# Denominators and variances of a fused attention and MLP kernel leave TensorE in short pieces on more rows

## The chip, the core and the metric

The kernel runs on one core of a Trainium2 chip. The metric is device time in microseconds (us). A core has five engines that run side by side, each through its own queue in order: TensorE (PE; its weight loads are shown apart, as PEld), VectorE (DVE), ScalarE (ACT), GpSimd (POOL) and SyncE (SP), which issues most of the DMA transfers.

## The reference

Three stages run one after the other on 4 batches of a sequence of 1088. First, linear attention with 4 heads of 32, whose features are the 64 products of two projections to 8:

```python
def phi(x):
    a = np.einsum('rd,bhsd->bhsr', S1, x)
    b = np.einsum('rd,bhsd->bhsr', S2, x)
    return np.einsum('bhsi,bhsj->bhsij', a, b).reshape(*x.shape[:-1], r * r)
q_p, k_p = (phi(q), phi(k))
kv = np.einsum('bhsf,bhsd->bhfd', k_p, v)
z = np.sum(k_p, axis=2)
num = np.einsum('bhsf,bhfd->bhsd', q_p, kv)
den = np.einsum('bhsf,bhf->bhs', q_p, z)[..., None] + 1e-06
return (num / den).astype(np.float32)
```

Second, on the 128 channels: a two-dimensional FFT, a layer norm and an MLP of 128 to 512 to 128.

```python
X = np.fft.fft(np.fft.fft(x, axis=1), axis=2)
u = x + np.real(X).astype(np.float32)
mu = np.mean(u, axis=-1, keepdims=True)
var = np.mean((u - mu) ** 2, axis=-1, keepdims=True)
un = (u - mu) / np.sqrt(var + 1e-06)
return u + np.maximum(un @ w_ch1, 0.0) @ w_ch2
```

Third, a gated MLP of 128 to 1024 to 128: `h = relu(x @ w_in)`, a convolution of three taps along the sequence, a sigmoid of it as the gate, and `(h * gate) @ w_out`.

## The kernel before

Channels lie on the 128 partitions and the sequence along the free axis, in pieces of 364, 364 and 360. Per batch the stages are `load_attn`, `attn`, `fft`, `moe1` and `moe2`; the loop over the batches stands at the end of `tile_fwd`. It runs nothing yet: each operation is only recorded (class `Program`, `record`), and `issue` then hands all of them to the engines in the order of a table of numbers, `ORDER`, lines 43 to 115. So every instruction of the profile has line 150, the call in `issue`, and rows are told apart by the names of their tiles. The table interleaves the batches: while one is in `moe2`, the next is in `attn` and `fft`. An engine runs its part strictly in that order, so an instruction that waits holds up all behind it.

Attention. `q`, `k` and `v` are loaded (`v` on 121 rows, since the sequence is cut into 9 tiles of 121), with weights and constants; 64-bit weights go through `load64`, which brings a `raw` tile of two shared slots and converts it to f32 in `em` on ACT and VectorE. `kab` and `qab` are the projections, `kp` and `qa` their products. In batch 0 the products of q are made from two wide projections (`sq_sb`) with three `acc` banks to share; in the others q's projections go through DRAM (`qd`) to be spread over the partitions. `kv_ps` sums keys times values, with a column of ones in `v` for the denominators' weights `z`. The denominators, `den`, are 8 matmuls of 32 rows by 273 columns, four column groups for the four quarters of the sequence; of every 32 rows, four (one for each head) hold a value. ACT adds eps (`rd`). In batch 0 VectorE takes the reciprocal of 128x273, and 4 matmuls with a selection matrix spread it over the partitions (`rb`). In batches 1 to 3 four transfers bring the 16 useful rows to 112x39 (`rr`), VectorE takes the reciprocal, one transfer writes it to DRAM (`rrd`) and four read it back, each head's over 32 partitions (`x`). Then `x` is multiplied by `num`.

Layer norm. `norm` in `moe1` squares the centred `u` (`cen`, `sq`), and 4 matmuls with `ones_v` give the variances, of which one row in 32 is needed (`var`); ACT takes the root (`rs`, 128x272). In batch 0 VectorE takes the reciprocal and GpSimd spreads it. In the others a transfer brings the four rows to 32x34 (`rt`), then comes the reciprocal, a transfer to DRAM (`rtd`) and one back over all partitions (`y`), which `down` multiplies into `ch`. From that come `yh` and `yl`, a value's upper part and its rest, which the matmuls `z` of `moe2` read.

`idle` are 48 matmuls on a tile of zeros (96 records, as an f32 matmul is recorded twice), which the table puts between the others.

## Time and profile before

| | us |
|---|---|
| median of 3 timed runs (267.41 to 267.97) | 267.42 |
| the profiled run | 265.54 |
| its span, in which the rows stand | 263.8 |
| TensorE busy | 254.1 (96%) |
| VectorE busy | 234.4 (89%) |
| ACT busy | 184.7 (70%) |
| GpSimd busy | 5.7 (2%) |

The profile is of one execution; its span runs from the first to the last instruction. PE is a matmul, PEld a weight load, which runs beside the matmuls. "x16" is a count of records. Idle time before a row stands in brackets with what ended it. A chain of waits is followed back from the last instruction.

### The profile page before, as it was taken

What the parts mean: (1) busy time and instruction counts of PE and PEld (TensorE: products, weight loads), DVE (VectorE), ACT (ScalarE), POOL (GpSimd) and SP (SyncE); (2) the same over time, 40 slices, a digit from 0 to 9 for tenths busy, and PEclk for the clock granted to TensorE, in tenths of its full rate; (3) what the DMA queues carried; (4) which work ended last, traced back from release to release, by engine and by line L of the source; (5) the groups of instructions that cost most, each with busy time, mean ns of one, the idle gap of its engine ahead of it and who ended that gap; (6) DMA issues with size and microseconds to landing.
All of it is one profiled execution on the core that took longest, in us unless ns stands there. A gap on an engine that the chain in (4) does not pass through costs nothing.

```text
span 263.8 us, 4314 instructions
## 1 busy us (share of the span) xinstructions
PE 254.1 (96%) x1644; PEld 198.5 (75%) x1644; DVE 234.4 (89%) x354; ACT 184.7 (70%) x330; POOL 5.7 (2%) x15
## 2 busy tenths in 40 slices
...
GB/s 234 276 388 306 178 188 209 155 207 214 107 130 262 65 14 120 0 132 126 79 10 2 60 0 87 97 20 0 0 2 28 1 40 105 0 0 28 59 0 85
DMA packets 9360, 26.48 MB, mean 100 GB/s; under 512 B 2360, under 2 KB 3896, under 8 KB 9084
## 3 DMA queue, kind: packets, MB, share of 16 engines
...
q0 software_dynamic: 400, 2.67, 3.0%
...
HBM read 23.00 MB, written 3.13 MB: 99 GB/s over the span
## 4 chain that ended last, share of the span: by engine, by line
PE 81%; DMA 9%; DVE 4%; ACT 4%; issue 1%; SPq 1%; ACTq 0%
PE z L150 27%; PE acc L150 18%; PE ch L150 11%; PE spec L150 4%; DVE t L150 4%; PE qab_ps L150 3%; PE kv_ps L150 3%; PE p_ps L150 3%; DMA v<-va 3%; PE num L150 3%; PE idle L150 2%; PE kab_ps L150 2%; DMA q<-qT 2%; DMA qd<-qab 2%; DMA raw<-w 2%; PE den L150 2%
## 5 line engine op out<-in xcount | busy, mean ns | idle before, releaser
L150 DVE SCALAR_TENSOR_TENSOR t<-h,cw_sb,t 128x1087 f32<-128x1087 f32 x64 | 83.6, 1339 | 0.8 <-ACT t L150 0.3
L150 PE MATMUL acc<-t,wo_sb 128*128 128x364 f32 (+1 forms) x192 | 68.8, 470 | 0.2 <-DVE t L150 0.2
L150 ACT ACTIVATE h<-z 128x364 f32<-128x364 f32 (+1 forms) x96 | 41.4, 474 | 16.7 <-PE z L150 16.0
L150 DVE TENSOR_TENSOR t<-t,h 128x1088 f32<-128x1088 f32 (+2 forms) x34 | 41.0, 1219 | 4.3 <-ACT t L150 4.2
L150 PEld LDWEIGHTS acc<-t,wo_sb 128*128 128x128 f32 x192 | 34.6, 189 | 11.3 <-issue 1.0
L150 ACT ACTIVATE t<-h,cw_sb 128x1088 f32<-128x1088 f32 x32 | 38.6, 1208 | 2.0 <-PE var L150 1.7
L150 ACT ACTIVATE t<-t 128x1088 f32<-128x1088 f32 (+2 forms) x34 | 35.5, 1056 | 4.1 <-DVE t L150 3.7
L150 PE MATMUL z<-yh,win_hi 128*128 128x364 f32 (+1 forms) x96 | 34.3, 382 | 0.0
L150 PE MATMUL ch<-hid,w_sb 128*128 128x364 f32 (+1 forms) x96 | 33.7, 470 | 0.0
L150 PE MATMUL z<-yh,win_lo 128*128 128x364 f32 (+1 forms) x96 | 33.1, 361 | 0.0
L150 PE MATMUL z<-yl,win_hi 128*128 128x364 f32 (+1 forms) x96 | 31.7, 350 | 0.0
L150 ACT ACTIVATE hid<-z 128x364 f32<-128x364 f32 (+1 forms) x48 | 21.7, 476 | 12.1 <-PE z L150 11.2
L150 PEld LDWEIGHTS ch<-hid,w_sb 128*128 128x128 f32 x96 | 17.2, 189 | 6.9 <-ACT hid L150 0.7
L150 PEld LDWEIGHTS z<-yh,win_hi 128*128 128x128 f32 x96 | 17.9, 188 | 4.8 <-ACT t L150 1.0
L150 PE MATMUL z<-uh,w_hi 128*128 128x364 f32 (+1 forms) x48 | 17.8, 395 | 2.3 <-ACT hid L150 2.3
L150 PEld LDWEIGHTS z<-yh,win_lo 128*128 128x128 f32 x96 | 18.0, 189 | 2.3
L150 PEld LDWEIGHTS z<-yl,win_hi 128*128 128x128 f32 x96 | 17.8, 188 | 1.8
L150 PEld LDWEIGHTS idle<-still 128*128 128x128 f32 x96 | 15.4, 214 | 4.1 <-issue 1.3
L150 PE MATMUL idle<-still 128*128 128x128 f32 x96 | 17.2, 305 | 1.2 <-DVE still L150 1.2
L150 PE MATMUL z<-uh,w_lo 128*128 128x364 f32 (+1 forms) x48 | 17.8, 377 | 0.0
L150 PE MATMUL z<-ul,w_hi 128*128 128x364 f32 (+1 forms) x48 | 16.5, 367 | 0.0
L150 PE MATMUL p_ps<-mats_sb,parts 128*32 128x128 f32 (+1 forms) x160 | 15.0, 277 | 0.0
(115 smaller groups left out, 388.2 us busy)
## 6 DMA issues: line engine op xcount, KB each, us to landing
...
v<-va SPq DMA_DIRECT2D x4, 561.5 KB
...
```

The lines of the kernel that those rows point to most:

```text
L150: fn(*args, **kw)
```

## The change

Rows that hold nothing are filled. A piece of the denominators' quarter (91 of 273 columns, `DJ = 3`) goes to its own row for each head: the weights `z` become a wider tile, in which the piece's window of 32 columns starts one column further left, and 24 matmuls add into the same 32 rows. Twelve of 32 rows then hold values, in 91 columns. `rd` and its reciprocal are 128x91 in all batches and go straight to DRAM; the four `rr` transfers are gone, and the four `x` transfers read three runs a quarter. In batch 0 the spreading takes 12 matmuls with three selection matrices, so `mats` grows from 320 to 448 KB. Likewise the variances of batches 1 to 3 take 16 matmuls of 68 columns (`VJ = 4`) with a shifted window of `one_v`; root and reciprocal are 128x68, and the `rt` transfer is gone. `v` is loaded on 128 rows (594 KB in place of 561.5), of which the matmuls still use 121. The idle matmuls are 24, and every number of `ORDER` is new.

```diff
-P = dict(near=(0,), kvt=(0, 1, 3), hs=(), hlo=4, xb=2, sq=(0,), rpe=(0,), rnear=(), up=(0,), mo=12, hid=7, idle=48)
+P = dict(near=(0,), kvt=(0, 1, 3), hs=(), hlo=4, xb=2, sq=(0,), rpe=(0,), up=(0,), mo=12, hid=7, idle=24)
...
+DJ = 3
+DW = QW // DJ
+VJ = 4
+ZW = 32 + DJ - 1
...
 ORDER = [
-    30, 31, 32, 33, 0, 1, 2, 3, 34, 4, 5, 85, 9, 6, 7, 8, 10, 16, 24, 14, 12, 35, 36, 37, 94, 91, 13, 23, 19, 83, 15, 22, 38, 95, 96, 25, 225, 87, 11,
...
+    72, 32, 33, 9, 0, 8, 63, 34, 35, 36, 67, 1, 73, 2, 37, 38, 39, 40, 41, 3, 42, 43, 4, 5, 6, 7, 19, 30, 16, 23, 61, 13, 15, 44, 11, 45, 74, 21, 191,
...
     ones_v = cst.tile([128, 32], F32, name="ones_v")
     V.memset(ones_v, 1.0 / D)
+    one_v = cst.tile([128, 63], F32, name="one_v")
+    V.memset(one_v, 0.0)
+    V.memset(one_v[:, 31:32], 1.0 / D)
     vks = []
     for i in range(2):
         vks.append(cst.tile([128, 128], F32, name=f"vk{i}"))
...
     kvz = []
     for i in range(2):
         t = cst.tile([128, 2, 64], F32, name=f"kv{i}")
-        z = cst.tile([128, 64], F32, name=f"z{i}")
+        z = cst.tile([128, 2 * ZW], F32, name=f"z{i}")
         V.memset(t, 0.0)
         V.memset(z, 0.0)
         kvz.append((t, z))
...
     def load_attn(b):
         k_sb[b] = at.tile([D, NKT * KT], F32, tag="k", name=f"k{b}")
         nc.sync.dma_start(k_sb[b], kT[b])
-        v_sb[b] = at.tile([KT, NKT, NH, HD + 1], F32, tag="v", name=f"v{b}")
+        v_sb[b] = at.tile([128, NKT, NH, HD + 1], F32, tag="v", name=f"v{b}")
         nc.sync.dma_start(v_sb[b], va[b])
         q_sb[b] = at.tile([D, SP], F32, tag="q", name=f"q{b}")
         nc.sync.dma_start(q_sb[b], qT[b])
-    mats_sb = cst.tile([D, 5, D], F32, name="mats_sb")
-    eye_sb, sel_sb, cen_sb, c_sb, s_sb = (mats_sb[:, i] for i in range(5))
+    mats_sb = cst.tile([D, 4 + DJ, D], F32, name="mats_sb")
+    eye_sb, cen_sb, c_sb, s_sb, *sel_sb = (mats_sb[:, i] for i in range(4 + DJ))
     tab_hi = cst.tile([128, 8, NK], F32R, name="tab_hi")
     tab_lo = cst.tile([128, 8, NK], F32R, name="tab_lo")
     tab_end = cst.tile([96, 4, NK], F32R, name="tab_end")
...
                     for hp in range(2):
                         T.matmul(
                             kv_ps[64 * hp:64 * hp + HD + 1, 64 * h2:64 * h2 + 64],
-                            vt[:, t, 2 * hp + h2, :],
+                            vt[:KT, t, 2 * hp + h2, :],
                             kp[hp][:, t, h2].rearrange("p i j -> p (i j)"),
                             start=(t == 0),
                             stop=(t == NKT - 1),
...
                     T.matmul(
                         kv_ps[:, hp * 66:(hp + 1) * 66],
                         kp[hp][:, t].rearrange("p h i j -> p (h i j)"),
-                        vt[:, t, 2 * hp:2 * hp + 2, :].rearrange("p h d -> p (h d)"),
+                        vt[:KT, t, 2 * hp:2 * hp + 2, :].rearrange("p h d -> p (h d)"),
                         start=(t == 0),
                         stop=(t == NKT - 1),
                     )
...
         for h2 in range(2):
             r = slice(64 * h2, 64 * h2 + 64)
             V.tensor_copy(kv[r, :, 32 * h2:32 * h2 + 32], kvv[h2][:, :, 0:32])
-            V.tensor_copy(zz[r, h2:h2 + 35:34], kvv[h2][:, :, 32])
+            V.tensor_copy(zz[r, DJ - 1 + DJ * h2:DJ + DJ * h2 + ZW + 2 * DJ:ZW + 2 * DJ], kvv[h2][:, :, 32])
         for hp in range(0 if b in P["sq"] else 2):
             V.tensor_tensor(qa[hp], qa[hp], qb[hp], op=ALU.mult)
         den = bank(f"den{b}", "mm")
         for hp in range(2):
             for c in range(4):
-                T.matmul(
-                    den[32 * c:32 * c + 32, :QW],
-                    zz[:, 32 * hp:32 * hp + 32],
-                    qa[hp][:, c * QW:(c + 1) * QW],
-                    start=(hp == 0),
-                    stop=(hp == 1),
-                )
-        rd = at.tile([128, QW], F32, tag="rd", name=f"rd{b}")
-        A.activation(rd, den[:, :QW], AF.Identity, bias=eps_d)
+                for j in range(DJ):
+                    o = ZW * hp + DJ - 1 - j
+                    T.matmul(
+                        den[32 * c:32 * c + 32, :DW],
+                        zz[:, o:o + 32],
+                        qa[hp][:, c * QW + j * DW:c * QW + (j + 1) * DW],
+                        start=(hp == 0 and j == 0),
+                        stop=(hp == 1 and j == DJ - 1),
+                    )
+        rd = at.tile([128, DW], F32, tag="rd", name=f"rd{b}")
+        A.activation(rd, den[:, :DW], AF.Identity, bias=eps_d)
+        V.reciprocal(rd, rd)
         x = xs[b] = ff.tile([128, SP], F32, tag="x", name=f"x{b}", bufs=P["xb"])
         xq = x.rearrange("p (c n) -> p c n", c=4)
         if b in P["rpe"]:
-            V.reciprocal(rd, rd)
             for c in range(4):
                 p = bank(f"rb{b}_{c}", "mm")
-                T.matmul(p[:, :QW], sel_sb[32 * c:32 * c + 32, :], rd[32 * c:32 * c + 32, :], start=True, stop=True)
+                for j in range(DJ):
+                    r = slice(32 * c, 32 * c + 32)
+                    T.matmul(p[:, j * DW:(j + 1) * DW], sel_sb[j][r], rd[r], start=True, stop=True)
                 A.copy(xq[:, c, :], p[:, :QW])
-        elif b in P["rnear"]:
-            V.reciprocal(rd, rd)
-            for c in range(4):
-                r = rd[32 * c:32 * c + NH, :]
-                nc.sync.dma_start(xq[:, c, :], r.unsqueeze(1).to_broadcast([NH, HD, QW]))
         else:
-            rr = at.tile([4 * NH * 7, QW // 7], F32, tag="rr", name=f"rr{b}")
+            rrd = dr.tile([128, DW], F32, tag="rrd", name=f"rrd{b}")
+            nc.sync.dma_start(rrd, rd)
             for h in range(NH):
-                nc.sync.dma_start(rr[28 * h:28 * h + 28, :], rd[h:h + 97:32, :])
-            V.reciprocal(rr, rr)
-            rrd = dr.tile([NH, SP], F32, tag="rrd", name=f"rrd{b}")
-            nc.sync.dma_start(rrd.rearrange("h (s n) -> (h s) n", n=QW // 7), rr)
-            for h in range(NH):
-                src = bass.AP(rrd.tensor, rrd.offset + h * SP, [[0, HD], [1, SP]])
-                nc.sync.dma_start(x[HD * h:HD * h + HD, :], src)
+                src = bass.AP(rrd.tensor, rrd.offset + h * DJ * DW, [[0, HD], [32 * DW, 4], [1, QW]])
+                nc.sync.dma_start(xq[HD * h:HD * h + HD], src)
         for i in range(3):
             n = bank(f"num{b}_{i}", "mm")
             for hp in range(2):
...
                 T.matmul(c[:, :w], cen_r, ul[:, o:o + w], start=False, stop=True)
                 A.activation(sq[:, o:o + w], c[:, :w], AF.Square)
             vp = bank(f"var{b}")
-            for c in range(4):
-                T.matmul(vp[32 * c:32 * c + 32, :VW], ones_v, sq[:, c * VW:(c + 1) * VW], start=True, stop=True)
-            rs = ln.tile([128, VW], F32, tag="rs", name=f"rs{b}")
-            A.activation(rs, vp[:, :VW], AF.Sqrt, bias=eps_d)
             if b in P["near"]:
+                for c in range(4):
+                    T.matmul(vp[32 * c:32 * c + 32, :VW], ones_v, sq[:, c * VW:(c + 1) * VW], start=True, stop=True)
+                rs = ln.tile([128, VW], F32, tag="rs", name=f"rs{b}")
+                A.activation(rs, vp[:, :VW], AF.Sqrt, bias=eps_d)
                 V.reciprocal(rs, rs)
                 yq = y.rearrange("p (c n) -> p c n", c=4)
                 for c in range(4):
                     G.partition_broadcast(yq[:, c, :], rs[32 * c:32 * c + 1, :])
             else:
-                rt = ln.tile([32, VW // 8], F32, tag="rt", name=f"rt{b}")
-                nc.sync.dma_start(rt, rs[0:97:32, :])
-                V.reciprocal(rt, rt)
-                rtd = dr.tile([32, VW // 8], F32, tag="rtd", name=f"rtd{b}")
-                nc.sync.dma_start(rtd, rt)
-                nc.sync.dma_start(y, bass.AP(rtd.tensor, rtd.offset, [[0, D], [1, SEQ]]))
+                n = VW // VJ
+                for c in range(4):
+                    for j in range(VJ):
+                        o = c * VW + j * n
+                        T.matmul(vp[32 * c:32 * c + 32, :n], one_v[:, 31 - j:63 - j], sq[:, o:o + n], start=(j == 0), stop=(j == VJ - 1))
+                rs = ln.tile([128, n], F32, tag="rt", name=f"rt{b}")
+                A.activation(rs, vp[:, :n], AF.Sqrt, bias=eps_d)
+                V.reciprocal(rs, rs)
+                rtd = dr.tile([128, n], F32, tag="rtd", name=f"rtd{b}")
+                nc.sync.dma_start(rtd, rs)
+                src = bass.AP(rtd.tensor, rtd.offset, [[0, D], [32 * n, 4], [1, VW]])
+                nc.sync.dma_start(y.rearrange("p (c n) -> p c n", c=4), src)
         up(0)
         norm()
...
-_SEL = np.kron(np.ones((4, 1)), np.kron(np.eye(32, NH), np.ones((1, HD)))).astype(np.float32)
+_SEL = [
+    np.kron(np.ones((4, 1)), np.kron(np.eye(32)[:, j:j + DJ * NH:DJ], np.ones((1, HD)))).astype(np.float32)
+    for j in range(DJ)
+]
...
+    vv = np.concatenate([vv, np.zeros((NB, 128 - KT) + vv.shape[2:], v.dtype)], axis=1)
...
-        "mats": np.concatenate([np.eye(D, dtype=np.float32), _SEL, _CEN, _C, _S], axis=1),
+        "mats": np.concatenate([np.eye(D, dtype=np.float32), _CEN, _C, _S, *_SEL], axis=1),
```

SyncE at the start, before (raw tiles hold 64-bit weights; w is that of the first MLP, twice, win that of the second):

```order
L150 DMA raw_78<-srep 128x16
L150 DMA q_108<-qT 128x1092
L150 DMA raw_109<-w 128x512
L150 DMA k_106<-kT 128x1089
L150 DMA raw_112<-w 128x512
L150 DMA v_107<-va 121x1188
L150 DMA mats_sb<-mats 128x640
L150 DMA raw_114<-win 128x512
L150 DMA q_259<-qT 128x1092
L150 DMA raw_116<-win 128x512
L150 DMA k_257<-kT 128x1089
```

SyncE at the start after:

```order
L157 DMA raw_110<-w 128x512
L157 DMA raw_78<-srep 128x16
L157 DMA q_109<-qT 128x1092
L157 DMA k_107<-kT 128x1089
L157 DMA raw_115<-win 128x512
L157 DMA mats_sb<-mats 128x896
L157 DMA v_108<-va 128x1188
L157 DMA raw_113<-w 128x512
L157 DMA k_258<-kT 128x1089
L157 DMA q_260<-qT 128x1092
L157 DMA raw_117<-win 128x512
```

w and srep, the vectors of the projections, have changed places; half of win has moved ahead of mats and v, and the second w behind v.

TensorE at the start, before, up to the first kv matmul:

```order
L150 MATMUL qab_ps_1_2_0_143<-q_108,sq_sb 128x364
L150 MATMUL idle<-still 128x128 x4
L150 MATMUL qab_ps_0_0_1_134<-q_108,sq_sb 128x364
L150 MATMUL qab_ps_0_2_0_137<-q_108,sq_sb 128x364
L150 MATMUL idle<-still 128x128 x2
L150 MATMUL qab_ps_1_2_1_144<-q_108,sq_sb 128x364
L150 MATMUL idle<-still 128x128 x3
L150 MATMUL qab_ps_0_2_1_138<-q_108,sq_sb 128x364
L150 MATMUL idle<-still 128x128
L150 MATMUL kv_ps_131<-kp_1_130,v_107 33x64
```

TensorE after, from its first matmul on; the row that follows is the first kv matmul:

```order
L157 MATMUL idle<-still 128x128 x13
L157 MATMUL qab_ps_0_0_0_134<-q_109,sq_sb 128x364
L157 MATMUL qab_ps_1_0_0_140<-q_109,sq_sb 128x364
L157 MATMUL kab_ps_0_128<-sab_sb,k_107 121x64 x5
L157 MATMUL qab_ps_1_0_1_141<-q_109,sq_sb 128x364
L157 MATMUL qab_ps_1_1_0_142<-q_109,sq_sb 128x364
L157 MATMUL kab_ps_0_128<-sab_sb,k_107 121x64 x3
L157 MATMUL qab_ps_0_1_0_136<-q_109,sq_sb 128x364
L157 MATMUL qab_ps_0_2_0_138<-q_109,sq_sb 128x364
L157 MATMUL kab_ps_1_129<-sab_sb,k_107 121x64
L157 MATMUL qab_ps_0_1_1_137<-q_109,sq_sb 128x364
L157 MATMUL qab_ps_1_2_0_144<-q_109,sq_sb 128x364
```

kv begins after eight of the twelve qab matmuls in place of all twelve, behind 13 idle matmuls at the start in place of eight.

TensorE at the end of moe1 of batch 0 and the beginning of moe2 (the z matmuls that read yh), before:

```order
L150 MATMUL ch_2_210<-hid_2_3_209,w_sb 128x360
L150 MATMUL z_0_0_364_217<-yh_175,win_hi 128x364
L150 MATMUL z_0_4_0_236<-yh_175,win_hi 128x364
L150 MATMUL z_0_4_0_236<-yh_175,win_lo 128x364
L150 MATMUL z_0_0_364_217<-yh_175,win_lo 128x364
L150 MATMUL z_0_0_364_217<-yl_176,win_hi 128x364
L150 MATMUL z_0_4_0_236<-yl_176,win_hi 128x364
L150 MATMUL kab_ps_1_400<-sab_sb,k_387 121x64
L150 MATMUL den_275<-qa_0_260,z_91 32x273 x4
L150 MATMUL den_275<-qa_1_261,z_91 32x273 x4
L150 MATMUL kv_ps_403<-v_388,kp_0_401 128x66 x2
L150 MATMUL z_0_0_0_216<-yh_175,win_hi 128x364
```

TensorE at the same place after:

```order
L157 MATMUL ch_2_211<-hid_2_3_210,w_sb 128x360
L157 MATMUL den_276<-qa_0_261,z_92 32x91 x12
L157 MATMUL den_276<-qa_1_262,z_92 32x91 x12
L157 MATMUL z_0_0_364_218<-yh_176,win_hi 128x364
L157 MATMUL z_0_0_0_217<-yh_176,win_hi 128x364
L157 MATMUL z_0_0_0_217<-yh_176,win_lo 128x364
L157 MATMUL z_0_0_0_217<-yl_177,win_hi 128x364
L157 MATMUL z_0_0_364_218<-yh_176,win_lo 128x364
```

den of batch 1 (den_275, den_276) has moved from behind six z matmuls of moe2 to ahead of the first.

ACT at the root of the variances (rs before, rt after) of batch 1, while moe2 of batch 0 runs, before (sq is the square for var, hid frees a bank of moe1's z, t is a copy of moe2's h):

```order
L150 ACTIVATE sq_314<-cen_728_317 128x360
L150 ACTIVATE sq_314<-cen_364_316 128x364
L150 ACTIVATE sq_314<-cen_0_315 128x364
L150 ACTIVATE t_7_250<-h_7_249,cw_sb 128x1088
L150 ACTIVATE hid_2_0_333<-z_1_2_0_332 128x360
L150 ACTIVATE hid_1_0_324<-z_1_1_0_323 128x364
L150 ACT_TABLE_LOAD
L150 ACTIVATE rs_319<-var_318,eps_d 128x272
```

ACT at the same place after:

```order
L157 ACTIVATE sq_314<-cen_728_317 128x360
L157 ACTIVATE sq_314<-cen_364_316 128x364
L157 ACTIVATE hid_2_0_332<-z_1_2_0_331 128x360
L157 ACTIVATE sq_314<-cen_0_315 128x364
L157 ACTIVATE hid_1_0_323<-z_1_1_0_322 128x364
L157 ACTIVATE t_6_246<-h_6_245,cw_sb 128x1088
L157 ACT_TABLE_LOAD
L157 ACTIVATE rt_319<-var_318,eps_d 128x68
L157 ACTIVATE t_7_251<-h_7_250,cw_sb 128x1088
L157 ACTIVATE hid_0_0_307<-z_1_0_0_306 128x364
```

The first two hid have moved ahead of a copy t and stand between the squares; a copy stands on either side of the table load and the root.

## Rows read from the trace of the kernel before

**Rows 1.** The page, parts 1 and 2: TensorE's busy time; GB/s by slice.

```profile
PE 254.1 (96%) x1644; PEld 198.5 (75%) x1644; DVE 234.4 (89%) x354; ACT 184.7 (70%) x330; POOL 5.7 (2%) x15
...
GB/s 234 276 388 306 178 188 209 155 207 214 107 130 262 65 14 120 0 132 126 79 10 2 60 0 87 97 20 0 0 2 28 1 40 105 0 0 28 59 0 85
```

**Rows 2.** Busy time by stretch: length, PE, PEld, DVE, ACT, POOL, clock, DMA share, GB/s.

```profile
0.00:64.20 64.20, 60.43 (x509) 48.01 (x509) 53.03 (x127) 29.01 (x69) 5.70 (x15) 1.00 0.82 237
64.20:104.00 39.80, 39.80 (x287) 33.04 (x286) 38.48 (x60) 28.46 (x49) 0.00 (x0) 1.00 0.46 124
104.00:110.00 6.00, 4.26 (x27) 2.10 (x26) 5.77 (x8) 3.45 (x7) 0.00 (x0) 1.00 0.00 0
110.00:223.00 113.00, 112.46 (x677) 88.46 (x675) 103.19 (x133) 93.00 (x158) 0.00 (x0) 1.00 0.16 46
```

**Rows 3.** Busy time by stretch, tile idle alone (columns PE, PEld, clock, DMA).

```profile
0.00:64.20 64.20, 15.54 (x88) 14.07 (x88) 1.00 0.82 237
64.20:104.00 39.80, 1.64 (x8) 1.31 (x8) 1.00 0.46 124
```

**Rows 4.** Time line, VectorE: start, length, instruction, idle before and its releaser.

```profile
82.16 1.42 DVE L150 TENSOR_TENSOR x<-num,x 128x364 f32<-128x364 f32 x3 [0.25 <-DMA x<-rrd]
```

**Rows 5.** VectorE by line and form: busy us, mean ns | idle before, releaser.

```profile
L150 DVE RECIPROCAL rd<-rd 128x273 f32<-128x273 f32 x1 | 1.8, 1849 | 0.0
...
L150 DVE RECIPROCAL rr<-rr 112x39 f32<-112x39 f32 x3 | 1.2, 394 | 0.0
...
L150 DVE RECIPROCAL rt<-rt 32x34 f32<-32x34 f32 x3 | 1.1, 353 | 3.4 <-DMA rt<-rs 3.4
...
L150 DVE MEMSET z<- 128x64 f32 x2 | 0.2, 112 | 0.0
```

**Rows 6.** The chain that ended last: start, length, what (TensorE).

```profile
9.44 0.80 PE kab_ps L150 x8
...
10.24 0.67 PE qab_ps L150 x2
...
42.97 2.21 PE kv_ps L150 x72
...
51.16 0.60 PE var L150 x8
...
65.74 1.06 PE den L150 x16
...
188.12 1.65 PE p_ps L150 x28
```

**Rows 7.** Time line, TensorE in the start.

```profile
1.17 3.79 PE L150 MATMUL idle<-still 128*128 128x128 f32 x16 [1.17 <-DVE still L150]
...
5.19 1.46 PE L150 MATMUL qab_ps<-q,sq_sb 128*128 128x364 f32 x4 [0.23 <-DMA q<-qT]
...
18.64 2.45 PE L150 MATMUL kv_ps<-kp,v 121*33 121x64 f32 x72
```

**Rows 8.** Time line near 106 us, ACT and TensorE.

```profile
106.68 1.20 ACT L150 ACTIVATE t<-h,cw_sb 128x1088 f32<-128x1088 f32 x1 [1.68 <-PE var L150]
...
108.29 0.43 PE L150 MATMUL z<-uh,w_hi 128*128 128x364 f32 x1 [1.74 <-ACT hid L150]
```

**Rows 9.** VectorE's wait for w_in, its releaser's own wait, and their stretch.

```profile
21.17 0.66 ACT L150 ACTIVATE em<-raw 128x512 f32<-128x512 f32 x1 [4.52 <-DMA raw<-win]
...
21.87 0.43 DVE L150 TENSOR_SCALAR em<-em 128x512 f32<-128x512 f32 x1 [0.99 <-ACT em L150]
...
4.90:23.00 18.10, 16.85 (x147) 12.63 (x146) 14.25 (x37) 7.04 (x19) 2.74 (x6) 1.00 1.07 343
```

**Rows 10.** The chain that ended last: loads of batch 1.

```profile
18.56 5.00 DMA q<-qT
...
34.56 8.28 DMA v<-va
```

**Rows 11.** Time line, SyncE: the first large load.

```profile
1.18 0.41 SPq L150 DMA_DIRECT2D q<-qT  x1
```

143 rows, old and new, of the table ORDER are left out of this document.

## The prediction, made before the changed kernel was run

> **What bounds the kernel now.** I read the page's busy times first, then the busy times by stretch, then the chain that ended last, then the time lines of the places that the change touches. TensorE is busy 254.1 of 263.8 us, VectorE 234.4, and the granted clock is 1.00 in every stretch, its upper level, 2.4 GHz [rows 1, 2]. But a share of 96% hides two things. First, 17.2 us of it are warm-up matmuls on a tile of zeros: 15.54 us of them lie before 64.2 us, the place where the second MLP of batch 0 begins, and 1.64 us in the 40 us after it [rows 3]. Second, between 64.2 and 223 us TensorE is without a pause but for one place: it is busy 39.80 of 39.80, then 4.26 of 6.00, then 112.46 of 113.00 us [rows 2]. So there are two regimes. Before 64.2 us the kernel waits for loads and for VectorE (53.03 busy of 64.20) and TensorE has some 19 us to spare (3.8 idle and 15.5 of zeros); there a TensorE instruction costs little, and a VectorE instruction or a late load costs its length. After 64.2 us TensorE is the bound: each microsecond put on it or taken from it counts, and a transfer made shorter counts only if TensorE waited for it.
>
> **The change, part by part.** All sums are against the profiled run of 265.54 us: its span of 263.8 and 1.74 around it. The median of the timed runs, 267.42, lies 1.88 above; I carry the difference in time over to it unchanged.
>
> *The transfers that go.* In batches 1 to 3 the four small rr transfers and their 39-column reciprocal become one reciprocal on 91 columns, and the rt transfer goes too. For batch 1 VectorE waited for the end of that chain, at 82.16 us, for a mere 0.25 us, with TensorE full [rows 4]. The rt transfer made VectorE wait 3.4 us in all [rows 5], but under a TensorE that is busy 112.46 of 113.00 us [rows 2]. What is late there next is TensorE's own queue. I take 0 for all of these; the far end is a gain of the 0.54 us that TensorE lacks in that stretch. A shorter chain lets the searched order move work, and that is costed below where it lands.
>
> *VectorE's reciprocals.* 273 columns took 1849 ns and 34 columns 353 ns [rows 5]: 1496 ns for 239 columns, 6.3 ns a column, so 91 columns come to 0.72 us and 68 to 0.57 us (estimates from these rows). Batch 0 wins 1.85 - 0.72 = 1.13 us in the start, where VectorE is on the path. Batches 1 to 3 lose 3 x (0.72 - 0.39) + 3 x (0.57 - 0.35) = 1.6 us, spread over the stretch where TensorE is the bound; VectorE has 1.3 us free from 64.2 to 104 and 9.8 from 110 to 223 [rows 2], so this is hidden at 0. Without that cover it would cost up to 1.6.
>
> *The pieces on TensorE.* The denominators of a batch become 24 matmuls in place of 8, the variances 16 in place of 4. Each leaves two records in the trace, one for each pass of f32: 48 in place of 16, 32 in place of 8. The columns streamed are the same, 8 x 273 and 4 x 272, and the pieces still alternate over the four column groups. Now 16 records of den take 1.06 us and 8 of var 0.60 [rows 6]. If only columns count, nothing is added. The nearest row with a narrow load before each short matmul is kv_ps, 33 columns loaded and 64 streamed: 72 records in 2.21 us, 0.031 each [rows 6]. At that price den is 48 x 0.031 = 1.47 (+0.41) and var 32 x 0.031 = 0.98 (+0.38). The far row is p_ps, 28 records in 1.65 us, 0.059 each, of which many use one column group or the full array [rows 6]: den 2.83 (+1.8), var 1.89 (+1.3). In the stretch that TensorE bounds stand the pieces of den 2 and 3 and var 1 to 3: 0 by columns, 2 x 0.41 + 3 x 0.38 = 2.0 by the kv_ps row, 2 x 1.8 + 3 x 1.3 = 7.5 by p_ps. The four groups of den overlap more than the two of kv_ps, so I take the middle of the lower two, **+1.0**.
>
> A rule speaks against the change. The row: kv_ps keeps a spacing of 31 ns with a load before each matmul [rows 6]. The Trainium skill, page "TensorE: Matmul & The Clock Gate", section "Back-to-back issue gap", gives about 81 ns as the sustained spacing of load and matmul pairs at 128 columns. By it the five places would cost 2 x (48 x 0.081 - 1.06) + 3 x (32 x 0.081 - 0.60) = 11.6 us, an estimate from that page; the row differs from it, and the sum goes by the row.
>
> *Batch 0's broadcast.* rb goes from 4 matmuls to 12 and rd0 from 273 to 91 columns. 16 more rb records at 0.1 us, the price of kab, full-width and short as they are (8 in 0.80 us) [rows 6], are 1.6 us at most, in the start, where TensorE has the time [rows 2, 3]: 0. Without that cover, +1.6.
>
> *den of batch 1.* Before, it stands behind the first six z matmuls of the second MLP, which begin at 64.2 us; it follows at 65.74 us for 1.06 us, on a TensorE that is full from then on [rows 2, 6]. In the changed order it stands ahead of the first z, in the stretch where TensorE waits for layer-norm results. **-1.1**, or 0 if TensorE has no gap just there. The warm-up matmuls that go after 64.2 us (four to two) I count as nothing, since the waits that they filled may remain.
>
> *The hole at 106 us.* After var of batch 1 TensorE waited 1.74 us for a bank that ACT's hid frees; ACT had waited 1.68 us, by the profile for var, and then ran the copy t of 1.20 us, which stood ahead of hid [rows 8]. It is the only wait of TensorE beyond half a microsecond from 64.2 to 223 us. In the new order two hid stand ahead of such a copy, but the copy, a table load and the root of var stand ahead of the next ones, so a later bank may be late. I take half of the 1.74: **-0.9** (bounds 0 and -1.7).
>
> *The start.* Here the new order changes most, and here are the widest bounds. (a) VectorE: -1.13 for the reciprocal, +0.2 for the two memsets of one_v (z's, 64 columns, took 112 ns each [rows 5]). (b) The first half of w_in moves from the eighth load to the fifth. ACT waited 4.52 us for a half of it and VectorE 0.99 us behind ACT [rows 9]; I take up to -1.0. (c) v comes on 128 rows instead of 121: 594 KB for 561.5, yet the 121-row v of batch 1 stands with 8.28 us in the chain where q, 546 KB on 128 rows, has 5.00 [rows 10].
>
> That row bears on a rule: the Trainium skill, page "DMA: Bandwidth & Descriptors", section "Why a DMA increments its semaphore by 16 and not by 1", says a transfer uses the largest number of engines up to 16 that divides its outermost sizes, which for 121 rows is 11 and for 128 rows 16. The 8.28 us agree in direction; an estimate from that page, 5.00 x (594 / 546), gives 5.4 us for the new v.
>
> (d) Against this, w now goes ahead of srep, whose vectors feed the first matmuls, and v goes behind half of w_in and a larger mats. Before, 16 idle records began at 1.17 and took 3.79 us; 26 now come to 6.2, so the queue itself reaches the first qab at about 7.3 us. Eight qab matmuls at 0.67 and nine kab at 0.20 [rows 6] then bring TensorE to v at about 14.5 us; kv began at 18.64 before [rows 7]. Up to the end of v 3.2 MB must land. The page's rates in its 6.6 us slices, 234, 276 and 388 GB/s [rows 1], carry 1.5 MB by 6.6 us and the other 1.7 at 276 to 388 GB/s in 4.3 to 6.1 us: v is there at 11 to 13 us, in time. If the tables, 2.6 MB on GpSimd's queue, take half of the bandwidth from 6.6 us, it is 15 to 19 us. Together: (a) -0.9, (b) up to -1.0, part of it lost to (d); I take **-1.0** for the start, with bounds of -2.5 (kv more than 3 us earlier, most of it kept) and +3.5.
>
> Sum: -1.0 - 1.1 + 1.0 - 0.9 = **-2.0**: a profiled run of 263.5 us, a median of **265.4 us**.
>
> **The rivals.** *Late loads, slower.* In the start the head of TensorE's queue after eight qab matmuls is kv, and behind it wait the other four and VectorE's work on them. If v lands after about 14.5 us, each microsecond is lost there, since den, num and the whole batch-0 chain follow. With v at 17.5 us the start is 3.0 longer instead of 1.0 shorter: 265.4 + 4.0 = 269.4 us. For it: the start's GB/s are already near the best of the page [rows 1], and w stands ahead of srep: q, the first large load before, was issued at 1.18 us and released TensorE at 5.19 [rows 7, 11], 4.0 us, so w and srep come at some 4.7 us and leave VectorE idle until then. Against: VectorE stood still for 3.85 of the 18.10 us from 4.9 us on anyway [rows 9], so it can make up some. It decides from v at about 15 us on.
>
> *Short pieces are dear, slower.* The price of p_ps holds: 7.5 instead of 1.0, so 265.4 + 6.5 = 271.9 us. For it stands only that row, against it the kv_ps row. The page's spacing named above would be this mechanism, only stronger.
>
> *Nothing is left, the same.* den of batch 1 finds no gap and the hole at 106 us moves to another bank: without these 2.0 us the time is 267.4 us. For it: where TensorE is full the order can only trade.
>
> **How the numbers follow.** A run of this kernel tells 0.2% from no change, 0.53 us: faster is below 266.9, slower above 267.95. Forecast 0.54, late loads 0.22, dear pieces 0.08, nothing left 0.16. The forecast's own range is 262.9 (start -2.5, pieces at 0) to 266.9. The range reaches from 263.0 to 269.8, over most of the late loads and up to the dear pieces. A little of the "nothing left" case lies on either side of its band: faster 0.55, same 0.15, slower 0.30.
>
> **What would show it.** In the trace of after: den x48 at 1.1 to 1.5 us in the chain, var x32 at 0.6 to 1.0; kv_ps of batch 0 before 15 us with no wait for v of over half a microsecond; the first z<-yh at about 63 us; no TensorE wait of over 1 us near 106 us; the end, from the last layer norm on, as long as before. The prediction is wrong if the first z<-yh comes later than 65 us (late loads), if den's 48 records take over 2 us (dear pieces), or if new waits of TensorE show between 64 and 223 us.

## The result: 261.04 us, below the range

| us | before | after |
|---|---|---|
| median of 4 timed runs | 267.70 (267.41 to 269.08) | 261.04 (260.92 to 262.08) |
| the profiled run | 265.54 | 261.13 |
| its span | 263.8 | 259.4 |

The ratio is 0.975, with a 95% interval of 0.971 to 0.979. The direction was forecast, the size was not: 6.7 us in place of 2.0, and the range began at 263.0. Of these 6.7 us the spans hold 4.4; the other 2.3 lie in how the two profiled runs stand to their medians.

Where the 4.4 us lie, busy time by stretch shows. Both programs are cut at the first z<-yh (the second MLP of batch 0) and where VectorE begins the last batch's yl. Before, then after (columns: stretch, its length, PE, PEld, DVE, ACT and POOL busy, granted clock, DMA share, GB/s):

```profile
0.00:64.16 64.16, 60.39 (x509) 47.97 (x509) 52.99 (x127) 28.97 (x69) 5.70 (x15) 1.00 0.82 237
64.16:222.91 158.75, 156.47 (x985) 123.57 (x984) 147.39 (x197) 124.96 (x212) 0.00 (x0) 1.00 0.23 64
222.91:263.80 40.89, 37.19 (x154) 26.97 (x152) 34.04 (x32) 30.73 (x50) 0.00 (x0) 1.00 0.08 28
```

```profile
0.00:63.70 63.70, 59.51 (x561) 46.37 (x561) 51.94 (x128) 28.71 (x69) 6.46 (x15) 0.97 0.77 241
63.70:217.52 153.82, 152.94 (x1103) 124.90 (x1099) 148.43 (x198) 125.14 (x212) 0.00 (x0) 1.00 0.27 68
217.52:259.40 41.88, 38.39 (x156) 27.27 (x154) 33.99 (x32) 29.74 (x49) 0.00 (x0) 1.00 0.08 27
```

The start is 0.46 shorter, though its granted clock was 0.97 in after, the middle is 4.93 shorter, and the end 0.99 longer, since the new order leaves some more of TensorE's work for it. Middle and end together went from 199.64 to 195.70, so -3.94. TensorE's busy time there fell from 193.66 to 191.33 (-2.33) and its idle time from 5.98 to 4.37 (-1.61).

Three time lines of TensorE in after answer to [rows 7] and [rows 8] (start, length, instruction, idle before and its releaser): the start, the first z, and the place of the old hole.

```profile
1.17 4.97 PE L157 MATMUL idle<-still 128*128 128x128 f32 x26 [1.17 <-DVE still L157]
8.17 2.55 PE L157 MATMUL qab_ps<-q,sq_sb 128*128 128x364 f32 x4 [2.03 <-DMA q<-qT]
...
12.15 1.44 PE L157 MATMUL qab_ps<-q,sq_sb 128*128 128x364 f32 x4
...
16.83 0.41 PE L157 MATMUL kv_ps<-kp,v 121*33 121x64 f32 x6
...
62.60 1.17 PE L157 MATMUL den<-qa,z 128*32 128x91 f32 x48
63.70 0.60 PE L157 MATMUL z<-yh,win_hi 128*128 128x364 f32 x2
...
104.81 0.68 PE L157 MATMUL var<-sq,one_v 128*32 128x68 f32 x32
105.42 0.60 PE L157 MATMUL z<-uh,w_hi 128*128 128x364 f32 x2
```

den of batch 1 starts at 62.60 and the first z at 63.70: 48 records in 1.10 us, where 16 took 1.06 [rows 6]. var of batch 1 starts at 104.81 and the z behind it at 105.42: 32 records in 0.61, where 8 took 0.60 [rows 6], and that z, which waited 1.74 us before [rows 8], does not wait. The only TensorE wait of over a fifth of a microsecond after the start is a new one, in the last rows of a list of waits by engine and releaser (total us, times, longest; the one of kv_ps lies in the start) and in the time line:

```profile
PE p_ps L157 <- ACT pe L157: 0.7, 1, 0.7
PE kv_ps L157 <- ACT vk L157: 0.3, 1, 0.3
PE z L157 <- DVE yl L157: 0.2, 1, 0.2
...
133.93 0.30 PE L157 MATMUL p_ps<-mats_sb,parts 128*32 128x128 f32 x1 [0.66 <-ACT pe L157]
```

Finally VectorE's reciprocals, which answer to [rows 5] (by line and form: busy us, mean ns | idle before):

```profile
L157 DVE RECIPROCAL rd<-rd 128x91 f32<-128x91 f32 x4 | 2.9, 715 | 0.0
...
L157 DVE RECIPROCAL rt<-rt 128x68 f32<-128x68 f32 x3 | 1.7, 567 | 0.0
```

They cost what was estimated (0.72 and 0.57), and the 3.4 us in which VectorE waited for rt are gone.

### The profile page after: what moved, and what is told of

It reads as the page before. It is cut to its first block, busy times and chain, and to the rows that moved or that the text cites. A ratio compares the mean times of both kernels' runs of the same rounds, so it can differ in the third digit from the quotient of the medians.

```text
span 259.4 us, 4622 instructions
## 1 busy us (share of the span) xinstructions
PE 250.8 (97%) x1812; PEld 198.5 (77%) x1812; DVE 234.4 (90%) x356; ACT 183.6 (71%) x330; POOL 6.5 (2%) x15
## 2 busy tenths in 40 slices
DMA packets 11557, 26.87 MB, mean 104 GB/s; under 512 B 2224, under 2 KB 6832, under 8 KB 11280
## 4 chain that ended last, share of the span: by engine, by line
PE 81%; DVE 10%; DMA 4%; ACT 2%; issue 1%; SPq 0%; ACTq 0%; DVEq 0%
PE z L157 25%; PE acc L157 20%; PE ch L157 10%; PE qab_ps L157 5%; DMA q<-qT 4%; PE spec L157 4%; PE kv_ps L157 4%; DVE t L157 4%; PE p_ps L157 3%; PE num L157 3%; PE kab_ps L157 2%; PE cen L157 2%; ACT t L157 1%; PE var L157 1%; DVE ch L157 1%
## 5 line engine op out<-in xcount | busy, mean ns | idle before, releaser
L157 PE MATMUL z<-yh,win_hi 128*128 128x364 f32 (+1 forms) x96 | 37.2, 414 | 0.0
L157 PE MATMUL z<-yl,win_hi 128*128 128x364 f32 (+1 forms) x96 | 34.1, 366 | 0.2 <-DVE yl L157 0.2
L157 PE MATMUL z<-yh,win_lo 128*128 128x364 f32 (+1 forms) x96 | 34.1, 359 | 0.0
L157 PE MATMUL z<-uh,w_hi 128*128 128x364 f32 (+1 forms) x48 | 19.2, 410 | 0.0
L157 PE MATMUL z<-uh,w_lo 128*128 128x364 f32 (+1 forms) x48 | 16.9, 358 | 0.0
L157 PEld LDWEIGHTS p_ps<-mats_sb,parts 128*32 128x32 f32 (+1 forms) x160 | 13.2, 142 | 2.2 <-ACT pe L157 0.9
L157 DVE TENSOR_TENSOR kp<-kab_ps,kb 121x512 f32<-121x512 f32 (+1 forms) x24 | 12.2, 546 | 0.5 <-ACT kb L157 0.5
```

The source lines that it names most:

```text
L157: fn(*args, **kw)
```

## The experiments

### Both kernels again

Before and after, unchanged.

> The kernel before, unchanged, run again, to see what lies between its profiled run of 265.54 us and its timed runs near 267.4 to 269. Theory 1: its runs scatter, and the profiled run was a good draw: the spans of these runs then reach from about 263.8 to 267 us, and a profile of a longer one shows the longer part in the start, before the second MLP of batch 0 begins at 64.2 us. Theory 2: profiling shortens nothing and the time around the span is longer in timed runs: the spans then all lie within 0.5 us of 263.8.

Measured: 267.0 us (ten runs from 264.82 to 269.87), 0.9993 of 19 other runs of before on that chip [0.994, 1.004]. Its profile, of a run with a granted clock of 1.00, has a start of 65.65, a middle of 158.73 and an end of 40.8 us: what follows the first z is the same within 0.1 us, and the start moves by 1.5. With a clock of 1.00 the ten runs took 264.8 to 267.0 us, and with 0.994 267.0 to 269.2. So two things scatter: the start, at the full clock too, and, in half of these runs, a stretch at the lower clock, with which a run is about 1.5 us longer.

> The kernel after, unchanged, run again beside the others of this call, as their measure. If its start scatters as that of before does (264.8 to 271.8 us over 19 runs), its runs reach from 260 to 266 us; if the new order also made the start steadier, they stay within 2 us of 261.

Measured: 263.46 us (261.52 to 263.83), ratio 0.982 [0.975, 0.989]; start 63.69, middle 154.21, end 41.80 in its profile. On this chip three of the four runs had a clock under 1.00 (0.998, 0.993 and 0.993).

> After, unchanged, for comparison on this chip: 261 to 263.5 us, ratio 0.975 to 0.985.

Measured: 261.09 us, ratio 0.976 [0.972, 0.980]. In three sets of runs the gain was 1.8 to 2.5%.

### One half alone: the pieces in the old order

```diff
-P = dict(near=(0,), kvt=(0, 1, 3), hs=(), hlo=4, xb=2, sq=(0,), rpe=(0,), up=(0,), mo=12, hid=7, idle=24)
+P = dict(near=(0,), kvt=(0, 1, 3), hs=(), hlo=4, xb=2, sq=(0,), rpe=(0,), up=(0,), mo=12, hid=7, idle=48)
...
 ORDER = [
-    72, 32, 33, 9, 0, 8, 63, 34, 35, 36, 67, 1, 73, 2, 37, 38, 39, 40, 41, 3, 42, 43, 4, 5, 6, 7, 19, 30, 16, 23, 61, 13, 15, 44, 11, 45, 74, 21, 191,
...
+    32, 33, 34, 35, 0, 1, 2, 3, 36, 4, 5, 87, 9, 6, 7, 8, 10, 16, 24, 14, 12, 37, 38, 39, 96, 93, 13, 23,
```

All of the changed code, with ORDER taken from before: each piece stands where its long matmul stood.

> The code after (24 and 16 short pieces, reciprocals on 128 rows, two hops fewer, v on 128 rows) in the order of before: each piece stands where its long matmul stood, one_v's memsets behind ones_v's, 48 warm-up matmuls. Theory 'order': the gain is the order's, and the pieces neither cost nor give much: 267.5 us, within 0.8 of before, den x48 at about 1.1 us in the chain, TensorE's hole of 1.7 us at 106 us still there. Theory 'pieces': the shorter chains and reciprocals carry half of the gain or more: 264.5 us or less, and the hole at 106 us shorter.

Measured: 266.73 us, ratio 0.999 [0.996, 1.002]. In this version pieces of one column group stand partly behind one another, and in the den of batch 1 and in a var they cost more (the chain of waits):

```profile
23.56 1.09 PE den L154 x46
...
66.74 1.27 PE den L154 x44
...
163.02 0.87 PE var L154 x32
```

So it was repeated with the four column groups strictly in turn.

> The code after in the order of before, once more, with the pieces of a batch's four column groups strictly in turn (in the first such kernel other engines' operations split the runs, and pieces of one column group stood behind one another: its den and var came to 5.96 and 2.83 us behind the first z<-yh, against 5.24 and 2.00 in before). Theory 'turns matter': den and var there fall back to some 5.3 and 2.1 us, and from the first z<-yh to the end 199.2 to 199.5 us pass, against 200.7 in that kernel and 199.6 in before; the median falls to 265.5 to 266. Theory 'price of a piece': they stay at 5.9 and 2.8.

Measured: 266.16 us (ten runs, 265.27 to 267.27), ratio 0.998 [0.996, 1.001]: no gain, although the hole shrinks. TensorE near 106 us, and where the last z begin:

```profile
105.84 0.68 PE L154 MATMUL var<-sq,one_v 128*32 128x68 f32 x32
106.86 0.43 PE L154 MATMUL z<-uh,w_hi 128*128 128x364 f32 x1 [0.33 <-ACT hid L154]
...
223.96 0.43 PE L154 MATMUL z<-yl,win_hi 128*128 128x364 f32 x1 [0.53 <-DVE yl L154]
```

The pieces and the missing transfers alone take the wait from 1.74 to 0.33 us, without a new order of hid. But the middle is 159.60 us long, 0.85 more than before. The last batch's layer norm shows where it is given back, before and then in this run (ACT, VectorE and SyncE's issue of the transfer):

```profile
211.37 0.49 ACT L150 ACTIVATE rs<-var,eps_d 128x272 f32<-128x272 f32 x1
...
215.34 0.33 SPq L150 DMA_DIRECT2D y<-rtd  x1
...
220.12 0.98 DVE L150 TENSOR_TENSOR ch<-ch,y 128x364 f32<-128x364 f32 x2
```

```profile
210.57 0.32 ACT L154 ACTIVATE rt<-var,eps_d 128x68 f32<-128x68 f32 x1
...
212.78 0.57 DVE L154 RECIPROCAL rt<-rt 128x68 f32<-128x68 f32 x1
...
214.92 0.38 SPq L154 DMA_DIRECT2D y<-rtd  x1
...
220.58 0.99 DVE L154 TENSOR_TENSOR ch<-ch,y 128x364 f32<-128x364 f32 x2 [1.17 <-DMA y<-rtd]
```

The root is ready at 210.89, but the reciprocal keeps its old place in VectorE's queue, behind four steps of t, and begins 1.9 us later; so y is issued only 0.42 us earlier than before, with a transfer less on the way. And y itself takes longer. Before, VectorE had it 4.78 us after its issue without waiting; here it has it after 5.66, having waited 1.17. The changed kernel reads y in four runs of 272 values a row in place of one of 1088, and the page counts 6832 packets under 2 KB in place of 3896. VectorE no longer waits 3.4 us for rt, but it waits 2.4 for y; its last yl comes late, and TensorE stands still for 0.53 us. In after ACT's root of the last batch ends at 204.91 and the reciprocal begins at 205.08.

### The other half alone: the new order with long matmuls

The code of before, each long matmul in the place of its last piece in the new ORDER, the rr and rt transfers right behind their sources, 24 idle matmuls.

```diff
-P = dict(near=(0,), kvt=(0, 1, 3), hs=(), hlo=4, xb=2, sq=(0,), rpe=(0,), rnear=(), up=(0,), mo=12, hid=7, idle=48)
+P = dict(near=(0,), kvt=(0, 1, 3), hs=(), hlo=4, xb=2, sq=(0,), rpe=(0,), rnear=(), up=(0,), mo=12, hid=7, idle=24)
```

> The code before (8 and 4 long matmuls, four rr and one rt transfer per batch, v on 121 rows, mats of 320 KB) in the order of after, 24 warm-up matmuls: the rr transfers stand right behind the rd copy and the rt transfer behind the root, and the long matmul stands where its last piece stood. Theory 'order': nearly all of the gain stays: 261 to 262.5 us. Theory 'pieces': the new order cannot be had without the shorter chains: VectorE waits for rr, rt, x or y, TensorE for VectorE, 264.5 us or more.

Measured: 272.31 us without the slowest of its four runs (276.19, the one profiled), ratio 1.022 [1.015, 1.029]; the clocks were 0.975 to 0.992. Two things are late in it: v on 121 rows, for which TensorE waits 3.96 us at 19.00, and the transfers. The next run takes the first away.

```diff
-        v_sb[b] = at.tile([KT, NKT, NH, HD + 1], F32, tag="v", name=f"v{b}")
+        v_sb[b] = at.tile([128, NKT, NH, HD + 1], F32, tag="v", name=f"v{b}")
```

> The long pieces, rr and rt transfers of before in the order of after (272.9 us with v on 121 rows), now with v on 128 rows. v on 121 rows cost the kernel after 3.5 us of span, all of it before the first z<-yh. Theory 'two separate costs': 269 to 270 us, the rest (some 8 us over after) lies behind the first z<-yh in VectorE's waits for rr and rt. Theory 'one feeds the other' (late loads and late chains meet): 265 us or less.

Measured: 271.18 us (four runs, clocks of 0.975 to 0.994), ratio 1.016 [1.009, 1.023]. The start is now 64.33 us long, but the middle 160.78, with TensorE busy for 155.40 of it: 5.38 us idle, where after has 0.88.

### Which chain the new order cannot bear

After, with one chain as before: first the denominators (8 long matmuls, rr), then the variances (4 long matmuls, rt).

```diff
-            rrd = dr.tile([128, DW], F32, tag="rrd", name=f"rrd{b}")
-            nc.sync.dma_start(rrd, rd)
+            rr = at.tile([4 * NH * 7, QW // 7], F32, tag="rr", name=f"rr{b}")
...
+                nc.sync.dma_start(rr[28 * h:28 * h + 28, :], rd[h:h + 97:32, :])
+            V.reciprocal(rr, rr)
```

> After with the denominators alone as before (8 long matmuls, rr transfers, 39-column reciprocal); variances stay short. Theory A (the rr chain is what the new order cannot bear): some 5 us above after, VectorE waits about 6.9 us for rr as in the run with both chains. Theory B (the rt chain is): within 1.5 us of after. Theory C (each bears about half of the 6.6 us): 3 to 4 us above.

Measured: the runs with a clock of 0.99 or more took 266.39 to 268.76 us, ratio 1.0005 [0.996, 1.005], and the others, at 0.966 to 0.986, up to 275.58: the whole gain is gone. The profile (span 264.6, start 63.91, middle 158.81, end 41.88) shows how. VectorE by line and form, then VectorE and TensorE near 70 us:

```profile
L151 DVE RECIPROCAL rr<-rr 112x39 f32<-112x39 f32 x3 | 1.2, 397 | 7.1 <-DMA rr<-rd 7.1
...
69.28 0.40 DVE L151 RECIPROCAL rr<-rr 112x39 f32<-112x39 f32 x1 [3.36 <-DMA rr<-rd]
70.61 0.48 DVE L151 TENSOR_TENSOR kp<-kab_ps,kb 121x128 f32<-121x128 f32 x2
...
71.23 0.40 PE L151 MATMUL z<-yh,win_hi 128*128 128x360 f32 x1 [2.00 <-DVE kp L151]
```

The reciprocal stands in VectorE's queue where the short one stands in after, right behind ACT's rd; but rr lands 3.36 us later than VectorE is there. kp stands behind it, and TensorE, whose z waits for a bank that kp frees, stops for 2.00 us. In before the same reciprocal came at 71.37 and waited for nothing: that order had left it room.

```diff
-                rs = ln.tile([128, n], F32, tag="rt", name=f"rt{b}")
-                A.activation(rs, vp[:, :n], AF.Sqrt, bias=eps_d)
-                V.reciprocal(rs, rs)
+                rs = ln.tile([128, VW], F32, tag="rs", name=f"rs{b}")
+                A.activation(rs, vp[:, :VW], AF.Sqrt, bias=eps_d)
+                rt = ln.tile([32, VW // 8], F32, tag="rt", name=f"rt{b}")
+                nc.sync.dma_start(rt, rs[0:97:32, :])
+                V.reciprocal(rt, rt)
```

> After with the variances of batches 1 to 3 alone as before (4 long matmuls, rt transfer, 34-column reciprocal); denominators stay short. A: within 1.5 us of after although VectorE waits some 4.8 us for rt. B: some 5 us above after. C: 3 to 4 us above.

Measured: 263.22 us (263.0 to 263.67), ratio 0.984 [0.978, 0.989]: 2.1 us above after on the same chip. VectorE waits 4.9 us for rt:

```profile
L152 DVE RECIPROCAL rt<-rt 32x34 f32<-32x34 f32 x3 | 1.1, 354 | 4.9 <-DMA rt<-rs 4.9
```

The middles of four runs, in this order: the pieces in the old order, the new order with both old chains (v on 128 rows), after with the old denominators, after with the old variances (columns as above).

```profile
63.78:223.38 159.60, 158.54 (x1157) 126.59 (x1155) 148.94 (x198) 124.28 (x212) 0.00 (x0) 1.00 0.25 63
...
64.33:225.11 160.78, 155.40 (x967) 124.47 (x963) 146.43 (x197) 125.57 (x212) 0.00 (x0) 0.99 0.25 63
...
63.91:222.72 158.81, 153.94 (x1039) 124.27 (x1035) 147.55 (x199) 125.62 (x212) 0.00 (x0) 1.00 0.26 65
...
64.22:219.57 155.35, 153.39 (x1031) 123.92 (x1027) 147.41 (x198) 124.77 (x212) 0.00 (x0) 1.00 0.26 66
```

Against the 153.82 us of after, the chain over rr costs 4.99 us and the one over rt 1.53, together 6.5, and with both in it was 6.96. After's own middle moved by 0.4 between its profiles (153.82 and 154.21).

### Single steps

v on 121 rows again, all else as in after:

```diff
-        v_sb[b] = at.tile([128, NKT, NH, HD + 1], F32, tag="v", name=f"v{b}")
+        v_sb[b] = at.tile([KT, NKT, NH, HD + 1], F32, tag="v", name=f"v{b}")
```

> The kernel after with v on 121 rows, as in before; nothing else is changed. Theory 'v': the 128-row load is what lets kv stand behind eight qab matmuls; v lands later, TensorE and VectorE wait for it before 20 us, and the later loads come later too: 263 to 266 us, with a wait of TensorE for v. Theory 'chains': v does not matter, and the 12 us between the long pieces in the new order and after come from the rr and rt chains: 261 to 262 us.

Measured: 265.7 us, ratio 0.990 [0.986, 0.994]. TensorE's time line:

```profile
17.77 0.61 PE L157 MATMUL kv_ps<-kp,v 121*33 121x64 f32 x6 [3.18 <-DMA v<-va]
18.31 2.80 PE L157 MATMUL qab_ps<-q,sq_sb 128*128 128x364 f32 x4
```

The first z<-yh comes at 67.29, 3.6 us later than in after, and nothing is lost behind it (span 263.2 for 259.7; in the medians it is 2.2 us). The smaller transfer, 561.5 KB for 594, takes longer: issued at 6.80, it frees TensorE at 17.77, where the larger one, issued at 6.97 in after's second profile, frees it at 15.34. That is 2.4 us. Behind the wait the clock fell, too: four records of qab took 2.80 us, where they took 1.49 in that profile. All ten runs had a clock of 0.985 to 0.994.

The loads in another order: the projections' vectors (srep) and q ahead of w.

```diff
-    72, 32, 33, 9, 0, 8, 63, 34, 35, 36, 67, 1, 73, 2, 37, 38, 39, 40, 41, 3, 42, 43, 4, 5, 6, 7, 19, 30, 16, 23, 61, 13, 15, 44, 11, 45, 74, 21, 191,
...
+    0, 63, 72, 32, 33, 9, 8, 34, 35, 36, 67, 1, 2, 37, 38, 39, 40, 41, 3, 42, 43, 4, 5, 6, 7, 19, 30, 16,
```

> The kernel after with the loads begun as in before: srep, q, w, k in place of w, srep, q, k; w's first step on ACT stands behind the six sq_sb copies and on VectorE behind the sab_sb copies. Theory 'start bound by the first loads': the first qab begins at about 6.2 us in place of 8.17, TensorE does not stand still for 2 us before it, its clock does not fall there (4 qab records took 2.55 us behind that wait, 1.4 elsewhere), and the whole start moves: 258.5 to 260 us. Theory 'start bound by VectorE': the loads and VectorE's conversions of the weights end where they ended: 260.5 to 262 us.

Measured: 261.25 us, 2.2 less than after on the same chip (263.46). The first qab begins at 6.14 us and the first kv at 14.88, but the first z stands at 63.59, as in after: the first loads do not bound the start. All its four runs had a clock of 0.998 or more. That it takes away scatter, not work, is likely, since after has 261.04 and 261.09 in its other sets of runs; four runs of each do not show it.

den of batch 1 back behind six z matmuls:

```diff
-    410, 693, 699, 697, 703, 700, 694, 698, 704, 701, 432, 433, 434, 1071, 695, 440, 436, 705, 411, 437, 129, 438, 441, 442, 453, 454, 455, 435, 439,
...
+    411, 437, 129, 438, 441, 442, 681, 687, 684, 690, 682, 688, 685, 691, 686, 692, 683, 689, 696, 702, 693, 699, 697, 703, 700, 694, 698, 704,
```

> The kernel after with the denominators of batch 1 (24 pieces and their copy on ACT) behind six z matmuls of the second MLP, where before has them, in place of ahead of the first. Theory 'den in a gap': TensorE waits for yh at that place without den, and den's 1.1 us come onto its full stretch: 262 us, 0.8 to 1.1 above the kernel after of this call. Theory 'no gap': the z matmuls begin 1.1 us earlier and nothing changes: within 0.3 us.

Measured: 263.25 us beside 263.46, which the medians do not tell apart. The time line does:

```profile
62.73 0.60 PE L153 MATMUL z<-yh,win_hi 128*128 128x364 f32 x2 [0.95 <-ACT yh L153]
```

A gap of 0.95 us opens where den stood, and den's 1.1 us then lie in the full stretch. The span, 260.1 for 259.7, hides part of it, since this start was 0.8 us shorter up to there: from the ch ahead of the gap to the end 200.9 us pass, and 199.7 in after's second profile.

Shorter pieces still, in the same order:

```diff
-DJ = 3
+DJ = 7
...
-VJ = 4
+VJ = 8
```

> The kernel after with pieces about half as long: 56 matmuls of 39 columns for a batch's denominators (112 records in place of 48), 32 of 34 columns for its variances (64 records in place of 32), and mats of 704 KB in place of 448. The columns streamed are the same. If only columns count: den about 1.1 us, var about 0.6, the time within 1 us of after. At the 0.031 us a record of kv_ps: den 3.5 us, var 2.0, and the time some 9 us longer (three den and three var on a full TensorE). At 0.010 us a record: den 1.15, var 0.65.

Measured: 272.1 us (269.03 to 277.1; clocks of 0.957 to 0.979). It is not for the pieces of den and var, which stay cheap (the chain, in the slowest run):

```profile
120.53 0.70 PE var L160 x56
...
149.84 1.09 PE den L160 x86
```

That is 0.0125 us a record at 34 columns and 0.0127 at 39. The time goes into the start (the clock row of the page, one digit for 6.9 us, and TensorE's time line):

```profile
PEclk9999555899999999999999999999999999999999
...
23.87 1.45 PE L160 MATMUL den<-qa,z 128*32 128x39 f32 x112 [0.70 <-DVE z L160]
27.25 2.09 PE L160 MATMUL qab_ps<-q,sab_sb 128*64 128x273 f32 x8 [1.94 <-DMA q<-qT]
...
31.70 5.37 PE L160 MATMUL rb<-rd,mats_sb 32*128 32x39 f32 x28
...
37.72 5.36 PE L160 MATMUL rb<-rd,mats_sb 32*128 32x39 f32 x28
```

Behind the second wait the granted clock fell to 0.5, 1.2 GHz, and stayed there for some 20 us, in which TensorE hardly paused; the first z<-yh comes only at 78.65 us, 15.0 later than in after. A large part of it is another piece of the same edit: batch 0's spreading now takes seven selection matrices, and its 56 records of rb took 10.7 us, 0.19 each, where after has 24 of 91 columns in 2.1. So the pieces that fill 32 rows, one column group after the other, are cheap; those of rb, which fill all 128 rows, are not. What the late q (behind a larger mats, it may be), the lower clock and rb cost apart from one another is not shown. That the run came out some 9 us longer, as the price of kv_ps would have it, is chance: den and var have another cost.

Before without the four warm-up matmuls that stand behind the first layer norm:

```diff
-P = dict(near=(0,), kvt=(0, 1, 3), hs=(), hlo=4, xb=2, sq=(0,), rpe=(0,), rnear=(), up=(0,), mo=12, hid=7, idle=48)
+P = dict(near=(0,), kvt=(0, 1, 3), hs=(), hlo=4, xb=2, sq=(0,), rpe=(0,), rnear=(), up=(0,), mo=12, hid=7, idle=44)
```

> The kernel before without the four warm-up matmuls that stand behind its first z<-yh (44 in place of 48). From the first z<-yh to the last yl 158.75 us pass in before. Theory 'each is paid': 157.9 to 158.0, that is 0.8 less (8 records in 1.64 us, half of which overlaps). Theory 'they fill waits': 158.7.

Measured: 266.65 us, ratio 0.997 [0.993, 1.001]; the middle, in the profile of a run of 269.28 us, is 158.58 us, 0.17 less than before. In the old order these matmuls filled waits.

After with three edits: the loads in the other order (srep, q, w, k), no warm-up matmul behind the first layer norm (two matmuls, which are four records), and the end in the order of before. The same kernel ran twice.

```diff
-P = dict(near=(0,), kvt=(0, 1, 3), hs=(), hlo=4, xb=2, sq=(0,), rpe=(0,), up=(0,), mo=12, hid=7, idle=24)
+P = dict(near=(0,), kvt=(0, 1, 3), hs=(), hlo=4, xb=2, sq=(0,), rpe=(0,), up=(0,), mo=12, hid=7, idle=22)
```

> The kernel after with three edits: the first loads as srep, q, w, k; the two warm-up matmuls behind the first z<-yh left out; and from the last yl on, all operations in the order in which before has them (that stretch takes 41.8 us in after and 40.9 in before). If each stretch keeps what it showed: 0.0 for the loads, though steadier, -0.4 for the two matmuls, -0.9 for the end: 259.7 to 260.2 us. If the end's length comes from what is left over for it (four records of acc more), it stays at 41.8 and the time at 260.6 to 261.

> After with the vectors of the projections loaded first, without the four warm-up matmuls behind the first layer norm and with the end in the old order. If the three edits bring something: 0.2 to 0.6 us under after on the same chip, fewer runs with a granted clock under 1.00. If not: within 0.2 us of it.

Measured: 260.85 us (0.979 [0.975, 0.983]) and 260.81 us (0.975 [0.971, 0.979]). The second time after ran beside it with 261.09: 0.3 us apart, inside the scatter of either, so it is not shown to be faster than after.

## Why the prediction was too high

Three steps failed. The distance from the profiled run to the median was carried over as a constant; that put the time outside the range, for with the profiled run as measured it would have come to 261.13 + 1.88 = 263.0 us, the range's lower end. The pieces were priced too high by 0.9 us. And the chains and the order were priced apart, so no term held what they give together: put back into the new order, the old chains cost 4.99 and 1.53 us of the middle.

**The sum, on the spans.** Forecast -2.0, measured -4.4.

| term | forecast | measured |
|---|---|---|
| start, to the first z | -1.0 | -0.46, and den of batch 1 is now in it |
| den of batch 1 leaves the full stretch | -1.1 | -1.1 (0.95 gap without it) |
| pieces, five places | +1.0 | +0.1 (2 x 0.04 + 3 x 0.01) |
| warm-up matmuls behind the start | 0 | -0.9 (1.64 to 0.76 busy) |
| TensorE's idle time, the hole included | -0.9 | -1.6 in middle and end (the hole -1.74) |
| not placed | | -0.4 |

The start's term is smaller than its scatter: the first z stood at 64.16 and 65.65 us in two profiles of before, at 63.70, 63.69 and 62.90 in three of after. The den pieces of batches 2 and 3 stand between records of p_ps and cannot be timed alone; 0.04 is the price of batches 0 and 1. And the hole was not the only wait of over half a microsecond between 64.2 and 223 us, as the prediction has it: 0.54 us at 166.61, before a z that hid frees, was a second, and it is gone too.

**The pieces: the term that was mis-sized.** The price was set between 0 and the spacing of kv_ps, 31 ns a record, on the ground that four column groups overlap more than two. In turn over four groups, 48 records took 1.10 us, 23 ns each at 91 columns, and with pieces of 34 and 39 columns the spacing still fell to some 12.5 ns. The lower end of the range, 0, was nearly the value. The 81 ns that the Trainium skill, page "TensorE: Matmul & The Clock Gate", section "Back-to-back issue gap", gives for pairs at 128 columns is not what these cost either: 23 ns at 91 columns, 19 at 68. The dear-pieces rival, with its 7.5, is out for den and var.

**Transfers at 0: right as a price, wrong as a ground.** Costed one at a time, with the old order around them, rr and rt were worth 0, and the run with the pieces in the old order bears that out (0.998), though not for the reason given: TensorE's queue was not all that was late there, VectorE also waited 2.4 us for the longer y transfer. But "a shorter chain lets the searched order move work" was then costed by the few places that could be seen. The runs with one chain put back measure it: 4.99 us of the middle hang on the chain over rr and 1.53 on that over rt, of which 3.99 and 1.08 are idle time of TensorE. The new order alone is 1.6% slower than before, the pieces alone no faster, both 2.5% faster. No term of the sum was for that; the hole (-0.9) and the warm-up matmuls (0) were its visible parts, and both were taken too small. The order can place an instruction early only where its operand is early: in the new order rr's reciprocal waits 3.36 us for its transfer, and in the old order the short reciprocal begins 1.9 us after its operand is there. The hole's other mechanism also failed: it was ascribed to where hid stands, yet in the old order of hid the wait already fell to 0.33. The "nothing is left" rival described the pieces alone, not the change.

**The start: small, and not for the loads.** den of batch 1 found its gap. VectorE's reciprocal became 1.13 us shorter, as forecast. kv_ps was forecast at before 15 us and came at 16.83, in a run in which q landed late behind w and srep: TensorE waited 2.03 us for it at 8.17, and its clock was low behind that. After's second profile, with a clock of 1.00, has both earlier:

```profile
7.70 1.46 PE L157 MATMUL qab_ps<-q,sq_sb 128*128 128x364 f32 x4 [1.65 <-ACT sq_sb L157]
...
15.34 0.38 PE L157 MATMUL kv_ps<-kp,v 121*33 121x64 f32 x6 [0.47 <-DMA v<-va]
```

Yet the first z stood at 63.69 there and at 63.70 in the first profile, and at 63.59 with q loaded first. So the late q cost nothing in the end, and the late-loads rival's step, that each microsecond by which kv comes after 14.5 us is lost, did not hold for the 2 us from kv at 14.88 (q first) to kv at 16.83. What bounds the start instead was not shown; VectorE, busy for 52 of the 63.7 us, is the likely one. v itself was a small wait at most (0 to 1.2 us in the profiles of the new order with 128 rows): on 121 rows TensorE waits 3.18 us and the first z comes 3.6 us later. This was the one step that the prediction left uncertain between two rows and a rule (the Trainium skill, page "DMA: Bandwidth & Descriptors", section "Why a DMA increments its semaphore by 16 and not by 1", by which a transfer uses the largest number of engines up to 16 that divides its outermost sizes, so 11 for 121 rows and 16 for 128). The run with 121 rows agrees with it in direction.

**The median: the largest step that failed.** 1.88 us between the profiled run and the median were carried over unchanged. They were not a constant: with the medians of the result the distance was 2.16 us for before and -0.09 for after, and that gave 2.3 of the 6.7 us. Part of it was luck of the draw. Over the 68 runs of before that were timed beside the experiments, pooled, the 26 with a clock of 0.999 or more have a median of 266.46 us, 0.9 above the profiled one. The other 42 carry a stretch at the lower level. Of after's 14 runs, 8 have 0.999 or more, with a median of 261.08. So at the full clock the change is worth 5.4 us, and the rest is that before falls lower more often. For the same reason the 0.53 us by which the prediction tells a change from none was too small: the 68 runs reach from 264.84 to 272.13 us. Why before falls to the lower clock more often was not separated. It is not the order alone: in the old order the changed code kept 0.997 or more in all of its ten runs, with the column groups in turn. v's 128 rows are a candidate. A run that had a low stretch, before without the warm-up matmuls, shows one right behind a wait of TensorE:

```profile
24.68 0.49 PE L147 MATMUL kvt_ps<-mats_sb,vk 128*128 128x128 f32 x2 [2.70 <-ACT vk L147]
...
26.57 2.05 PE L147 MATMUL den<-qa,z 128*32 128x273 f32 x16
```

**The signs named ahead.** den x48 in 1.10 us and var x32 in 0.61, the first z at 63.70 (63 forecast), no wait near 106 us: right. kv_ps before 15 us (16.83) and an end as long as before (+0.99, work moved there): wrong. A new wait of TensorE between 64 and 223 us was named as a sign against the prediction, and there is one, of 0.66 us at 133.93; it is smaller than the 2.28 us of waits that went.

**Open.** TensorE's busy time in the middle rose by 2.07 us with the pieces in the old order, while den and var themselves did not. Some 0.5 of it is the cut: the middle ends where VectorE begins yl, which came late, and four records that stood behind it (0.53 us of the end) now stand before it. The other 1.5, and the 0.4 us above, have no place.
